# Tile 0's attention scores as plain float32 products over 64 rows, with a new table of priorities

## The chip, the cores and the metric

The kernel runs on one core of a Trainium2 chip. Five engines work side by side, each through its own instruction stream in order: TensorE (PE, with its weight loads PEld), VectorE (DVE), ScalarE (ACT), GpSimd (POOL) and SyncE (SP, which here only issues DMA transfers). The metric is the device time of one execution in microseconds (us).

## What is computed

Attention over 2 batches, 8 heads, 576 positions and 64 dimensions, in which every query keeps its 32 largest scores, and then two MLPs over the 1152 rows of 512 numbers. Everything is float32.

```python
scores = scale * np.matmul(q, k.transpose(0, 1, 3, 2))
kth = np.partition(scores, -32, axis=-1)[..., -32:-31]
scores = np.where(scores >= kth, scores, -1000000000.0)
attn = softmax(scores);  x = attn @ v          # per head, then (1152, 512)
h = x @ w_in;  g = h * tanh(softplus(h));  x = g @ w_out     # first MLP, d_ff 2048
x = (x @ w_a) * (x @ w_b) @ w_out                            # second MLP, d_ff 1536
```

## The kernel before

**Tiles.** The 1152 queries are nine tiles of 128; tile 4 holds the last 64 of each batch. A tile's attention is done for two heads at a time, a *pair* here: four pairs a tile, 36 in all, so pair 16 is the last of tile 3 and pair 26 the second of tile 6.

**Scores.** q and k come from memory transposed and twice over, in rows 0 to 63 and again in rows 64 to 127. A float32 product is made of two faster products in the format float32r: `prep_k` casts a head's k to float32r (line 347) and replaces rows 64 to 127 by what the cast lost (a subtraction, line 352), which gives the tile `kk`; `prep_q` makes `qh`, the cast of a pair's q, and `ql`, what it lost. `qh` times `kk` plus `ql` times `kk`, over 128 rows, is the score (line 468); each head is done in two halves of 288 columns, in a PSUM tile `psc`. ACT scales it into SBUF (line 473). Casts may go to ACT or DVE, subtractions to POOL or DVE.

**Search.** `largest` finds the 32 largest of 576 scores on DVE: for each of the two heads four times MAX8 (line 487) and between them three times MATCH_REPLACE8 (line 491), 8 and 6 instructions for a pair. Then ACT makes the masked exponentials (lines 530 and 533), PE transposes them (line 544, `pe`), ACT copies them, and PE multiplies them with v (lines 556 and 560, `px`).

**Weights.** They come as 64-bit numbers, 68 pieces (512 KB each). ACT takes one half of each word (line 624), ACT or POOL the other (lines 629, 631), POOL or DVE shift and add (lines 637 to 643), and the result is kept and also stored for a second use.

**MLPs.** Tiles 0, 1 and 2 go through the first MLP alone in plain float32 (`single`, products `ph` on line 784, then `acc` on line 714); tiles 3 to 5 and 6 to 8 in threes, with weights and activations split into two float32r parts (`gated`, lines 691, 712, 714); the second MLP (`bilinear`) goes in threes. Between the products of the first MLP stands `gate`: ACT, a minimum on POOL or DVE (line 745), three ACT steps and a DVE step (line 751).

**Order.** The program is a list of operations with priorities (`ATT`, `CONV`, `MLP`, `BIAS`). A planner (`Plan.run`) goes through a model of the engines, gives every free engine the ready operation with the smallest priority, chooses an engine where two are allowed (with the offsets `SHIFT` and `LOCKED`), and emits every engine's stream in that order. On the chip each stream is then followed to the letter: an instruction whose input is late holds up all behind it.

**What the change touches.** `RAW` names the tiles whose scores are done without `prep_q` and `prep_k`; the code for it is there, and the tuple is empty. `since` says at which tile a batch's k is prepared, the first that is not in `RAW`.

```python
since = [next(t for t in range(J + 1) if t not in RAW), J]
nc.tensor.matmul(psc()[:, :HS], QQ[t]()[:D, 2 * hp + s, :],
                 KR[b, hp]()[:D, s, a * HS:(a + 1) * HS], start=True, stop=True)
```

Of the kernel before, what the change touches and what calls it, by code (L numbers as in the profile page):

```python
# [26 lines left out]

SEQ = [(1, (0,), 0), (1, (1,), 0), (1, (2,), 0), (2, (0, 1, 2), 1), (1, (3, 4, 5), 1), (2, (3, 4, 5), 1),
       (1, (6, 7, 8), 1), (2, (6, 7, 8), 1)]
ATT = (-95.1, -36.4, 51.3, 93.5, 275.2, 298.4, 324.7, 574.5, 287.8, 2117.2)  # L30
CONV = (-156.2, -1.4, 50.6, 349.2, 528.4)
MLP = ((60.7, 126.0, -326.6, 1269.9), (97.8, 294.8, 551.3, -22.1), (-647.9, -146.1, -100.4, 111.3), (358.9, 501.8),
        (675.0, -3.6), (808.8, 2780.7), (965.3, 651.3), (-178.3, 7.5))
BIAS = {'scores': -43.1, 'search': 54.2, 'weigh': 49.7, 'gate': -708.6, 'conv': -16.9, 'load': 116.8, 'split':
        -23.9, 'x': -164.4, 'k': -304.6, 'prod': -25.3, 'acc': -7.7, 'out': -162.6, 'store': 620.6, 'v': 1161.1,
        'px': -671.5, 'mask': 337.5, 'turn': -20.1, 'tail': -26.6, 'last': 3.3, 'rest': 181.1}
FRESH = 200
RAW = ()
KEEP = (2, 2, 2, 2, 3, 3, 3, 3)
AHEAD = 1500.0  # L40
SLACK = 2500.0
# [25 lines left out]
class Plan:  # L67
# [11 lines left out]
    def add(self, engines, prio, fn, reads=(), writes=(), also=()):  # L79
        o = Op()  # L80
        o.engines, o.prio, o.fn, o.index = engines, round(prio, 3), fn, len(self.ops)
        o.need, o.bufs = set(), []
        touched = dict.fromkeys(also)
        for b, part in reads:
            for z in ([part] if part is not None else list(b.last)):
                if z in b.last:
                    o.need.add(b.last[z])
                elif None in b.last:
                    o.need.add(b.last[None])
                b.read.setdefault(z, []).append(o.index)  # L90
            if part is not None and None in b.last:
                o.need.add(b.last[None])
            touched[b] = None
        for b, part in writes:
            for z in ([part, None] if part is not None else list(b.last)):
                if z in b.last:
                    o.need.add(b.last[z])
            for z in ([part] if part is not None else list(b.read)):
                o.need.update(b.read.pop(z, []))
            if part is None:  # L100
                b.last.clear()
            b.last[part] = o.index
            touched[b] = None
        for b in touched:
            if not b.users:
                b.loaded = "SP" in engines
            b.users += 1
            o.bufs.append(b)
        o.need.discard(o.index)
        self.ops.append(o)  # L110
        return o
# [158 lines left out]

LAG = {"PE": 200.0, "DVE": 135.0, "ACT": 150.0, "POOL": 110.0, "SP": 2400.0}
START = {"PE": 900.0, "DVE": 900.0, "ACT": 2000.0, "POOL": 1700.0, "SP": 720.0}
SHIFT = {'DVE': -13.3, 'POOL': -36.4, 'ACT': 1362.4, 'PE': 0, 'SP': 0}
LOCKED = 720.9


def ramp(knots, z):
# [6 lines left out]
def topk_attention_mlps(ctx: ExitStack, tc: tile.TileContext, q, k, v, vr, w, out):  # L284
# [23 lines left out]
    add = plan.add  # L308
# [130 lines left out]
    def scores(t, hp, at):  # L439
        pr = at + BIAS["scores"]  # L440
        if hp == 0:
# [165 lines left out]
    for t, hp in steps:  # L607
        at = ATT[t] + (ATT[t + 1] - ATT[t]) * hp / NP
        s2 = scores(t, hp, at)
# [7 lines left out]
    for u, key in enumerate(order):  # L617
        pr = ramp(CONV, u / len(order)) + BIAS["conv"]
        w64 = buf("wp", [P, U], mybir.dt.int64, "w64", CAPS["w64"])
# [121 lines left out]
    def gate(pr, ph, full, N):  # L741
        e, g = buf("ep", [P, N], F32, f"e{N}", CAPS["ep"]), buf("ep", [P, N], F32, f"m{N}", CAPS["ep"])
        add(one("ACT", 75.0 + 0.83 * N), pr, lambda _: nc.scalar.activation(e(), ph()[:, :N], AF.Exp), full, [(e, 0)])
        add({"POOL": (95.0 + 1.22 * N, True), "DVE": (70.0 + 0.52 * N, True)}, pr,
            lambda z: ENG[z].tensor_scalar(e(), e(), TOP, None, op0=ALU.min), [(e, 0)], [(e, 0)])  # L745
        for cost, dst, fn, kw in ((110, e, AF.Square, {"bias": 1.0}), (200, e, AF.Ln, {"bias": half, "scale": 0.5}),
                                  (110, g, AF.Exp, {"scale": -1.0})):
            add(one("ACT", cost + 0.84 * N), pr,
                lambda _, dst=dst, fn=fn, kw=kw: nc.scalar.activation(dst(), e(), fn, **kw), [(e, 0)], [(dst, 0)])  # L749
        add(one("DVE", 65.0 + 1.04 * N), pr,  # L750
            lambda _: nc.vector.scalar_tensor_tensor(g(), g(), 1.0, ph()[:, :N], op0=ALU.subtract, op1=ALU.mult),
            full + [(g, 0)], [(g, 0)])
        return g
# [15 lines left out]
    def single(z, t, y):  # L769
        base = lambda f: MLP[z][0] + (MLP[z][1] - MLP[z][0]) * f / F1  # L770
        pre = lambda i: MLP[z][2] + (MLP[z][3] - MLP[z][2]) * i / (NC * FB)
        after = lambda c: ready(t, c - 1) if c else ready(t - 1) if t else []
# [24 lines left out]
    def gated(z, tiles, ys, direct):  # L797
        n = len(tiles)
        T = n * P
        base = lambda f: MLP[z][0] + (MLP[z][1] - MLP[z][0]) * f / F1  # L800
        xt = [buf("xp", [P, NC, T], F32R, f"x{y}{T}") for y in "hl"]
# [142 lines left out]
```

## Time and profile before

| | |
|---|---|
| median of 3 runs | 655.56 us (655.47 to 656.84) |
| the profiled execution | 654.66 us, its span 652.9 us |
| PE, PEld busy | 605.6, 532.8 us |
| DVE, ACT, POOL busy | 562.2, 470.5, 446.6 us |
| search on DVE, lines 487 and 491 | 205.0 and 159.1 us |
| `ph`, `po` and `acc` of the threes on PE, lines 691 and 714 | 231.8, 80.9, 85.5 us |

The span runs from the first to the last instruction of the profiled execution; 1.8 us of its own time lie around it. A busy PE is not a PE at its peak, since matmuls overlap and their ends are modelled; how close two starts stand tells its pace. A MAX8 and the next instruction overlap a little too, so that sums are made from durations only where the same kinds are compared.

### The profile page before, as it was taken

The numbers are of one execution on the slowest core, as the hardware profiler recorded it, in microseconds if no ns is written. First come the engines' busy times: TensorE is split into PE (matmuls) and PEld (weight loads), VectorE is DVE, ScalarE is ACT, GpSimd is POOL, SyncE is SP. The second block draws the span as 40 slices with busy tenths as digits, with TensorE's granted clock in tenths as the row PEclk, the third lists the DMA queues.
The fourth block names the chain that finished last, engine by engine and source line by source line (L and its number), as shares of the span: only waits on it lengthen the run. The fifth ranks groups of instructions, "written<-read, shape, count | busy, mean of one in ns | idle before, by whom it ended". The sixth has DMA issues, their size and how long they took to land.

```text
span 652.9 us, 12119 instructions
## 1 busy us (share of the span) xinstructions
PE 605.6 (93%) x4000; PEld 532.8 (82%) x4000; DVE 562.2 (86%) x1104; ACT 470.5 (72%) x1045; POOL 446.6 (68%) x485
## 2 busy tenths in 40 slices
PE   1488779999899999999999999999999999999997
PEld 1377646966757999898998997889999999999996
DVE  6999989989999999999999999997865788755552
ACT  4687899898999989998899789866542666432221
POOL 6999999988789999999887886453422566521110
PEclk9999899999999999999999999999999999999999
DMA  8887868978998755565753343133324444434401
GB/s 330 309 272 230 289 188 288 327 257 265 335 316 272 259 166 169 184 210 163 227 157 118 100 126 106 42 98 98 113 73 145 154 130 130 130 113 122 125 30 48
DMA packets 64719, 117.71 MB, mean 180 GB/s; under 512 B 6800, under 2 KB 23312, under 8 KB 64656
## 3 DMA queue, kind: packets, MB, share of 16 engines
q1 hardware_dynamic: 64512, 116.81, 55.4%
q8 instruction: 31, 0.51, 0.3%
q14 instruction: 32, 0.26, 0.1%
q10 hardware_dynamic: 144, 0.13, 0.1%
HBM read 96.73 MB, written 20.19 MB: 179 GB/s over the span
## 4 chain that ended last, share of the span: by engine, by line
PE 63%; DVE 15%; POOL 9%; ACT 6%; issue 3%; DMA 3%; SPq 0%; POOLq 0%; DVEq 0%; ACTq 0%
PE ph L691 30%; PE po L714 11%; DVE arena L487 6%; DVE arena L491 5%; PE acc L714 5%; PE acc L712 4%; PE psc L468 3%; PE pe L544 3%; PE px L556 3%; POOL arena L643 3%; PE ph L784 2%; ACT arena L347 2%; POOL arena L639 2%; DMA arena<-in_k_dram 1%; POOL arena L631 1%
## 5 line engine op out<-in xcount | busy, mean ns | idle before, releaser
L352 POOL TENSOR_TENSOR arena<-arena,arena 128x512 fp32r<-128x512 f32 (+3 forms) x192 | 221.3, 1164 | 151.4 <-ACT arena L347 97.2
L691 PE MATMUL ph<-arena 128*128 128x384 f32 x1248 | 231.8, 337 | 1.4 <-DVE arena L833 0.8
L691 PEld LDWEIGHTS ph<-arena 128*128 128x128 f32 x1248 | 216.9, 188 | 5.0 <-DVE arena L833 1.1
L487 DVE MAX8 arena<-arena 128x8 f32<-128x576 f32 x288 | 205.0, 745 | 2.4 <-ACT arena L473 1.8
L491 DVE MATCH_REPLACE8 arena<-arena 128x576 f32<-128x576 f32 x216 | 159.1, 740 | 0.1
L347 ACT CAST arena<-arena 128x512 fp32r<-128x512 f32 (+4 forms) x204 | 109.5, 558 | 51.0 <-PE ph L691 19.6
L352 DVE TENSOR_TENSOR arena<-arena,arena 128x512 fp32r<-128x512 f32 (+4 forms) x110 | 88.2, 802 | 11.8 <-ACT arena L347 8.1
L468 PE MATMUL psc<-arena 128*128 128x288 f32 x320 | 71.3, 343 | 22.3 <-POOL arena L352 14.9
L714 PE MATMUL acc<-arena 128*128 128x512 f32 x240 | 85.5, 478 | 4.5 <-issue 3.0
L643 POOL TENSOR_TENSOR arena<-arena 128x512 int32<-128x512 int32 x63 | 82.8, 1317 | 2.5 <-DVE arena L637 0.5
L714 PE MATMUL po<-arena 128*128 128x512 f32 x324 | 80.9, 394 | 0.0
L468 PEld LDWEIGHTS psc<-arena 128*128 128x128 f32 x320 | 51.0, 200 | 36.0 <-POOL arena L352 17.3
L347 DVE CAST arena<-arena 128x512 fp32r<-128x512 f32 (+2 forms) x98 | 52.2, 535 | 29.9 <-PE po L714 11.4
L714 PEld LDWEIGHTS po<-arena 128*128 128x128 f32 x324 | 59.5, 188 | 11.4 <-issue 0.3
L639 POOL TENSOR_TENSOR arena<-arena,eight 128x512 uint32<-128x512 uint32 x61 | 63.7, 1050 | 5.0 <-ACT arena L624 4.1
L749 ACT ACTIVATE arena<-arena 128x384 f32<-128x384 f32 (+1 forms) x88 | 48.2, 553 | 25.8 <-POOL arena L745 18.6
L530 ACT ACTIVATE arena<-arena 128x576 f32<-128x576 f32 x72 | 55.2, 783 | 9.8 <-DVE arena L487 8.8
L473 ACT ACTIVATE arena<-psc 128x288 f32<-128x288 f32 x144 | 54.4, 420 | 6.1 <-PE psc L468 5.4
L533 ACT ACTIVATE arena<-arena 128x576 f32<-128x576 f32 x72 | 56.0, 782 | 3.2 <-POOL arena L526 3.2
L784 PEld LDWEIGHTS ph<-arena 128*128 128x128 f32 x384 | 47.9, 200 | 8.9 <-DVE arena L581 5.7
L784 PE MATMUL ph<-arena 128*128 128x128 f32 x384 | 50.2, 286 | 3.9 <-DVE arena L581 3.4
L544 PEld LDWEIGHTS pe<-ident,arena 128*128 128x128 f32 x324 | 39.7, 145 | 16.3 <-ACT arena L533 6.5
(57 smaller groups left out, 698.6 us busy)
## 6 DMA issues: line engine op xcount, KB each, us to landing
arena<-ws SPq DMA_DIRECT2D x140, 256.0 KB, 2.7
arena<-in_w_dram SPq DMA_DIRECT2D x68, 512.0 KB, 5.1
ws<-arena SPq DMA_DIRECT2D x52, 256.0 KB, 5.2
arena<-wsa SPq DMA_DIRECT2D x48, 256.0 KB, 3.3
wsa<-arena SPq DMA_DIRECT2D x16, 256.0 KB, 5.2
arena<-in_q_dram SPq DMA_DIRECT2D x8, 512.0 KB, 5.4
arena<-in_k_dram SPq DMA_DIRECT2D x7, 576.0 KB, 4.4
arena<-in_v_dram SPq DMA_DIRECT2D x4, 512.0 KB, 6.8
```

The costliest lines, as they stand in the source:

```text
L347: add(eng, prio, lambda e: nc.scalar.copy(dst(), src()) if e == "ACT" else nc.vector.tensor_copy(dst(), src()), reads, writes)
L352: lambda e: ENG[e].tensor_sub(dst(), a(), b()), reads, writes)
L468: nc.tensor.matmul(psc()[:, :HS], z()[:, s, :], kk()[:, a * HS:(a + 1) * HS], start=(i == 0), stop=(i == len(heads) - 1))
L487: lambda e, s=s, src=src, got=got: nc.vector.max(m8()[:, s, got], src()[:, s, :]),
L491: lambda e, s=s, src=src, got=got: nc.vector.match_replace(wk()[:, s, :], m8()[:, s, got], src()[:, s, :], NEG),
L533: lambda e, s=s: nc.scalar.activation(e2()[:, s, :], e2()[:, s, :], AF.Exp, scale=-STEEP, bias=dm()[:, s - 2 + n:s - 1 + n], accum_out=at_ ...
L544: nc.tensor.transpose(pe()[:, i * P:(i + 1) * P], ef[:, n * P:(n + 1) * P], ident)
L639: nc.gpsimd.tensor_tensor(wi().bitcast(U32), wi().bitcast(U32), eight.to_broadcast([P, U]), op=ALU.mult)
L643: lambda e, word=word, wi=wi: ENG[e].tensor_tensor(wi(), wi(), word(I32, 0), op=ALU.add),
L691: nc.tensor.matmul(ph()[:, o:o + T], a, x, start=(i == 0), stop=(i == len(mm) - 1))
L714: nc.tensor.matmul(acc[i](), z[:, i * P:(i + 1) * P], a, start=begin, stop=end)
L784: nc.tensor.matmul(ph()[:, j * P:(j + 1) * P], wa()[:, j * P:(j + 1) * P], x()[:, c, :], start=(c == 0 and j == 0), stop=(c == NC - 1 and ...
```

## The change

Tile 0's scores are made as one plain float32 product over rows 0 to 63 of q and k as they lie (line 458), instead of two float32r products over 128 rows. So tile 0 needs no `qh`, `ql` and `kk`. The k of batch 0 is loaded in two halves, rows 0 to 63 for tile 0 and rows 64 to 127 for `prep_k`, which now belongs to tile 1; the raw k of batch 0 stays in four tiles of their own. Of tile 0's q only rows 0 to 63 are loaded. The planner's price of the minimum on POOL (line 745) rises from 95 + 1.22 to 100 + 2.27 ns a column, and all priorities are new.

```diff
-ATT = (-95.1, -36.4, 51.3, 93.5, 275.2, 298.4, 324.7, 574.5, 287.8, 2117.2)
+ATT = (-57.5, -46.3, 47.6, 83.9, 224.8, 264.3, 487.1, 592.9, 528.3, 2195.4)
...
-RAW = ()
+RAW = (0,)
...
-SHIFT = {'DVE': -13.3, 'POOL': -36.4, 'ACT': 1362.4, 'PE': 0, 'SP': 0}
-LOCKED = 720.9
+SHIFT = {'DVE': 30.3, 'POOL': -17.2, 'ACT': 2219.2, 'PE': 0, 'SP': 0}
+LOCKED = 972.4
...
-        add({"POOL": (95.0 + 1.22 * N, True), "DVE": (70.0 + 0.52 * N, True)}, pr,
+        add({"POOL": (100.0 + 2.27 * N, True), "DVE": (70.0 + 0.52 * N, True)}, pr,
             lambda z: ENG[z].tensor_scalar(e(), e(), TOP, None, op0=ALU.min), [(e, 0)], [(e, 0)])
```

`CONV`, `MLP` and `BIAS` change in the same way as `ATT`.

In the rows that follow, `arena_81` is SBUF in float32 and `arena_82` SBUF in float32r; the line number tells the step. DVE at the start of the program, before:

```order
L347 CAST arena_82<-arena_81 128x576
L352 TENSOR_TENSOR arena_82<-arena_81,arena_82 64x576
L347 CAST arena_82<-arena_81 128x256
L352 TENSOR_TENSOR arena_82<-arena_81,arena_82 128x256
L637 TENSOR_SCALAR arena_81<-arena_81 128x512
L487 MAX arena_81<-arena_81 128x8
L347 CAST arena_82<-arena_81 128x256
L491 MATCH_REPLACE arena_81<-arena_81 128x576
L487 MAX arena_81<-arena_81 128x8 x2
```

and now:

```order
L487 MAX arena_81<-arena_81 128x8
L491 MATCH_REPLACE arena_81<-arena_81 128x576
L487 MAX arena_81<-arena_81 128x8 x2
L491 MATCH_REPLACE arena_81<-arena_81 128x576
L352 TENSOR_TENSOR arena_82<-arena_81,arena_82 64x576
L491 MATCH_REPLACE arena_81<-arena_81 128x576
L487 MAX arena_81<-arena_81 128x8
L352 TENSOR_TENSOR arena_82<-arena_81,arena_82 64x576
L347 CAST arena_82<-arena_81 128x576
L487 MAX arena_81<-arena_81 128x8
L491 MATCH_REPLACE arena_81<-arena_81 128x576
L352 TENSOR_TENSOR arena_82<-arena_81,arena_82 64x576
```

The search comes first; five of the eight subtractions of k (64x576), of which three are shown, and one of its casts now stand inside the first pair's search; the fourth stands ahead of its sixth MAX8, the fifth ahead of its seventh. ACT at the start of the program, before; the copies from `psc` are the scaled scores, the casts of 128x576 are k:

```order
L347 CAST arena_82<-arena_81 128x576
L347 CAST arena_82<-arena_81 128x256
L624 ACTIVATE arena_81<-arena_81 128x512
L473 ACTIVATE arena_81<-psc 128x288 x3
L624 ACTIVATE arena_81<-arena_81 128x512
L473 ACTIVATE arena_81<-psc 128x288
L629 ACTIVATE arena_81<-arena_81 128x512
```

and now:

```order
L473 ACTIVATE arena_81<-psc 128x288 x4
L347 CAST arena_82<-arena_81 128x576
L473 ACTIVATE arena_81<-psc 128x288
L347 CAST arena_82<-arena_81 128x576
L473 ACTIVATE arena_81<-psc 128x288
L347 CAST arena_82<-arena_81 128x576
L473 ACTIVATE arena_81<-psc 128x288 x3
L347 CAST arena_82<-arena_81 128x576
L473 ACTIVATE arena_81<-psc 128x288 x2
L347 CAST arena_82<-arena_81 128x576
L473 ACTIVATE arena_81<-psc 128x288 x2
L624 ACTIVATE arena_81<-arena_81 128x512
```

Behind these rows come three more copies, a sixth cast of k, a piece of weights (line 624) and a seventh cast of k. So all four pairs' scores of tile 0 and seven of the eight casts of k stand in a row, where before the first pair's four copies were followed by weights. SP's transfers at the start of the program, the difference:

```order
-L341 DMA arena_81<-in_k_dram 128x576 x2
-L341 DMA arena_81<-in_q_dram 128x768
+L341 DMA arena_81<-in_k_dram 64x576 x2
+L341 DMA arena_81<-in_q_dram 64x768
+L341 DMA arena_81<-in_k_dram 64x1152 x3
+L341 DMA arena_81<-in_k_dram 64x576 x2
+L341 DMA arena_81<-in_k_dram 64x1152 x3
 L341 DMA arena_81<-in_w_dram 128x512 x4
```

The whole k of batch 0, in ten loads of 64 rows, now stands ahead of the first four pieces of weights; before, three quarters of it came behind them.

## Rows read from the trace of the kernel before

**Rows 1.** Windows: stretch, length, busy PE, PEld, DVE, ACT, POOL (instructions), clock, DMA, GB/s.

```profile
0.00:100.00 100.00, 64.47 (x431) 51.14 (x432) 90.54 (x188) 75.99 (x164) 89.06 (x106) 0.98 0.81 271
...
225.00:653.00 428.00, 421.20 (x2730) 389.73 (x2728) 349.88 (x666) 281.23 (x630) 246.97 (x240) 1.00 0.41 127
```

**Rows 2.** Timeline: start, duration, engine, line; ends of pairs 16 and 26, their transposes.

```profile
205.35 0.75 DVE L487 MAX8 arena<-arena 128x8 f32<-128x576 f32 x1
...
204.76 4.26 PE L691 MATMUL ph<-arena 128*128 128x384 f32 x23 [0.19 <-DVE arena L738]
208.94 0.55 PE L544 MATMUL pe<-ident,arena 128*128 128x128 f32 x3
...
318.31 0.76 DVE L487 MAX8 arena<-arena 128x8 f32<-128x576 f32 x1
...
324.17 1.14 PE L544 MATMUL pe<-ident,arena 128*128 128x128 f32 x9
```

**Rows 3.** Timeline of the first 45 us, DVE, POOL and PE.

```profile
4.35 0.46 DVE L347 CAST arena<-arena 128x576 fp32r<-128x576 f32 x1 [3.44 <-DMA arena<-in_k_dram]
...
8.95 0.76 DVE L487 MAX8 arena<-arena 128x8 f32<-128x576 f32 x1 [0.17 <-ACT arena L473]
...
21.03 0.75 DVE L487 MAX8 arena<-arena 128x8 f32<-128x576 f32 x1
...
8.55 0.75 POOL L631 TENSOR_SCALAR arena<-arena 128x512 int32<-128x512 uint32 x1
...
37.35 5.49 PE L784 MATMUL ph<-arena 128*128 128x128 f32 x24 [2.09 <-DVE arena L581]
...
43.81 1.05 PE L784 MATMUL ph<-arena 128*128 128x128 f32 x8
```

**Rows 4.** DMA issues: transfer, queue, count, size, median us from issue to landing.

```profile
arena<-in_q_dram ACTq DMA_DIRECT2D x1, 128.0 KB, 3.8
```

**Rows 5.** The chain that ended last, in time: start, us, group.

```profile
122.25 3.57 PE ph L784 x32
...
144.06 1.72 PE acc L714 x4
...
235.56 2.10 PE ph L691 x12
```

**Rows 6.** Groups by line and shape: count, busy us, mean ns, idle before.

```profile
L473 ACT ACTIVATE arena<-psc 128x288 f32<-128x288 f32 x144 | 54.4, 420 | 6.1 <-PE psc L468 5.4
...
L352 DVE TENSOR_TENSOR arena<-arena,arena 128x512 fp32r<-128x512 f32 x66 | 46.6, 706 | 5.2 <-ACT arena L347 2.0
...
L352 DVE TENSOR_TENSOR arena<-arena,arena 128x384 fp32r<-128x384 f32 x29 | 29.2, 1008 | 6.2 <-ACT arena L347 6.1
...
L855 DVE TENSOR_TENSOR arena<-ph,arena 128x384 f32<-128x384 f32 x36 | 19.8, 551 | 22.1 <-PE ph L691 20.8 <-ACT arena L533 0.9
...
L352 POOL TENSOR_TENSOR arena<-arena,arena 64x576 fp32r<-64x576 f32 x9 | 12.9, 1433 | 5.8 <-ACT arena L347 4.5 <-POOL arena L745 0.5 <-POOL arena L352 0.4
...
L352 DVE TENSOR_TENSOR arena<-arena,arena 64x576 fp32r<-64x576 f32 x7 | 6.5, 922 | 0.2
...
L347 DVE CAST arena<-arena 128x576 fp32r<-128x576 f32 x9 | 5.2, 589 | 3.5 <-DMA arena<-in_k_dram 3.4
L347 ACT CAST arena<-arena 128x576 fp32r<-128x576 f32 x7 | 4.6, 676 | 5.8 <-DMA arena<-in_k_dram 5.8
L745 DVE TENSOR_SCALAR arena<-arena 128x512 f32<-128x512 f32 x7 | 4.6, 665 | 1.0 <-ACT arena L743 1.0
L352 DVE TENSOR_TENSOR arena<-arena,arena 128x256 fp32r<-128x256 f32 x6 | 4.2, 707 | 0.0
```

**Rows 7.** DVE's waits from 20 to 330 us: us in total, times, longest.

```profile
DVE arena L571 <- POOL arena L569: 1.7, 1, 1.7
DVE arena L751 <- ACT arena L749: 1.6, 2, 1.2
```

**Rows 8.** DMA from 511 to 520 us: GB/s in 40 slices.

```profile
GB/s 0 0 0 0 0 0 328 364 391 82 0 0 0 25 200 237 287 371 408 276 273 200 264 328 373 200 36 18 0 0 0 0 0 0 0 0 173 155 264 391
```

More of the change, by code (lines that the diff above doesn't have):

```diff
@@ L29 @@
        (1, (6, 7, 8), 1), (2, (6, 7, 8), 1)]
-ATT = (-95.1, -36.4, 51.3, 93.5, 275.2, 298.4, 324.7, 574.5, 287.8, 2117.2)
[L31 to L36, printed above, removed]
+ATT = (-57.5, -46.3, 47.6, 83.9, 224.8, 264.3, 487.1, 592.9, 528.3, 2195.4)
+CONV = (-140.8, -86.9, 24.7, 360.8, 543.5)
+MLP = ((-40.1, 108.8, -575.7, 1231.5), (242.2, 338.3, 237.0, -38.4), (-815.0, -200.1, -416.0, 215.1), (330.5,
+        577.2), (822.0, -59.3), (853.8, 2338.1), (555.5, 390.4), (-120.5, -19.1))
+BIAS = {'scores': -62.1, 'search': 66.5, 'weigh': 33.0, 'gate': -840.9, 'conv': -48.4, 'load': -341.5, 'split':
+        -64.5, 'x': -151.1, 'k': -594.8, 'prod': 27.2, 'acc': 36.1, 'out': -108.6, 'store': 555.4, 'v': 1257.1,
+        'px': -641.9, 'mask': 1083.0, 'turn': -16.7, 'tail': -0.1, 'last': -0.2, 'rest': 556.3}
 FRESH = 200
-RAW = ()
+RAW = (0,)
 KEEP = (2, 2, 2, 2, 3, 3, 3, 3)
```

## The prediction

> **What bounds the kernel now.** I read the windows first, then the timeline at the ends of searches, then the start.
>
> The windows show where time is lost [rows 1]. In the first 100 us PE is busy for 64.5, from 225 us on for 421.2 of 428. DVE is busy for 90.5 of the first 100. So PE is the bound of the later two thirds, and what it did not get to do in the front is missing at the end.
>
> The timeline shows where DVE sets PE's pace [rows 2]. The search of pair 16 ends at 205.35 + 0.75 = 206.1; PE works on `ph` right up to 208.94 and then starts the transposes of that pair, 2.8 us after the search. Between them lie two ACT passes over each head, so I take 2.8 as about the least there can be: here DVE and PE meet. At pair 26 the search ends at 319.1 and the transposes start at 324.17, 5.1 later: 2.3 us of slack. From the start of pair 16's transposes to the end it is 652.9 - 208.9 = 444.0 us. In the orders of both kernels PE's instructions from that point to the end are the same in number, kind for kind (1224 `ph` of 384 columns, 324 `po`, 192 and 144 `acc`, 160 `psc`, 189 transposes and the small ones). From pair 26 on the new order has six `psc` products fewer. So the change in time is the change in when DVE ends these searches, less slack, as long as PE is not later for reasons of its own.
>
> **The change part by part.** I call X the change of the end of the first pair's search, now at 21.03 + 0.75 = 21.8 [rows 3].
>
> *The products of tile 0.* Sixteen float32 products of 288 columns come, 32 float32r ones go. A float32 product is two records in the trace: 32 records of 128 columns take 3.57 us, 111 ns each, and 4 of 512 take 1.72, 430 each [rows 5]; 288 columns lie at about 244, so 0.49 us a product. The float32r products are bounded from above by those of 384 columns, 2.10/12 = 0.175 [rows 5], and 288/384 of that is 0.13. PE's work grows by 16 x 0.49 - 32 x 0.13 = 3.6 us. It all lies in the first 20 us, where PE waits for most of the time [rows 1], and costs nothing; without that cover it costs 3.6. [...]
>
> *The start of the search.* Before, k lands, DVE casts it at 4.35, and after cast, subtraction, product and copy MAX8 starts at 8.95 [rows 3]. Now the first product waits for half of k's first head and a load of q, issued at 0.8 and about 3.8 us under way [rows 4]: 4.6. Two products at 0.98, 0.2 for the end of the second (an estimate) and one copy of 0.42 [rows 6]: MAX8 starts at 7.2. The pair's own search is (205.0 + 159.1)/36 = 10.1 by the profile table. Into it the new order puts five subtractions of k at 0.92 and one cast at 0.59 [rows 6], 5.2 us. Without a wait it ends at 22.5: X = +0.7.
>
> *Waits in it.* The fourth subtraction in DVE's stream needs a cast that stands on ACT behind all 16 copies, five other casts and one piece of weights. DVE gets to it after 10 of 14 search steps, three subtractions and a cast, 7.2 + 7.2 + 3.4 = 17.8. ACT, never held up, has done it at 5.8 + 16 x 0.42 + 7 x 0.68 = 17.3 [rows 6]: no wait. [...] X lies between +0.7 and +4.3. ACT's first cast, after the fourth copy at 9.1, needs rows 64 to 127 of k, behind 1.4 MB of 64-row loads. The trace has two 64-row stores at about 515.3 to 516.2 us; in these slices 276, 273, 200 and 264 GB/s move, 371 and 408 ahead of them [rows 8], about 0.6. At 245 GB/s the rows land at 10.2 and hold ACT for 1.1, and DVE for 0.6. I take 0.7 for all waits, so **X = +1.4**.
>
> [...]
>
> *The rest of DVE's work.* Counted in the two orders, between the first pair and pair 16 two casts of k (0.59), one subtraction of q (0.71) and one of k (0.92) go, a minimum (0.67) and a short cast (0.3, an estimate) come [rows 6]: -1.9 us. Between the first pair and pair 26 three such casts and the two subtractions go (-3.4), two subtractions of 128x384 (1.01) and two of 128x512 (0.71), a minimum and a gate product (0.55) come (+4.7), and short casts and differences add 0.3: +1.5.
>
> *The other queues.* SP issues eleven loads ahead of the weights instead of three. POOL's first weight step, at 8.55 [rows 3], moves behind three subtractions of k (1.43 each) and, by the loads, to about 16. The first `ph` products ran at 37.35 [rows 3]; a delay of 7.5 us is covered if POOL converts four pieces in the 21 us that are left. Were it not, PE would start later by what is missing; it has 35 us of idle time in the front to absorb it. POOL later has two subtractions of k and three minima less, so it catches up. v lands at about 22 and is wanted behind the first transposes, at 26. The dearer minimum moves three of 44 from POOL to DVE; those that matter are counted above. Four output copies move from DVE to ACT, where neither is the bound: nothing.
>
> *The sum.* At pair 16: X - 1.9 = -0.5. At pair 26: X + 1.5, less 0.8 for six `psc` products that PE no longer has behind it, less the slack of 2.3: X - 1.6 = -0.2. The larger decides: -0.2. The profiled execution took 654.66, its span 652.9, and the median is 0.9 above it; I take the change from the median: **655.4**. With X at its ends it is 654.7 to 658.3, waits elsewhere aside.
>
> **The rivals.**
>
> *Faster: DVE's waits go too.* Up to pair 26 DVE waits for a reciprocal behind POOL (1.7) and twice for ACT's gate (1.6) [rows 7]. POOL has less to do and the gate's minimum moves to DVE, which speaks for it; that the streams are all new, and may bring waits like these elsewhere, against it. With X = +0.7 and one or both waits gone it is -0.9 - 1.6 to -0.9 - 3.3, so 651.4 to 653.1, at the middle 652.2. It decides if pair 16's transposes start before 207.6.
>
> [...]
>
> *Slower: the new work shows.* If PE does not fill the front better than before, because weights come late or scores wait for casts, it is not DVE that sets the pace, and the 3.6 us come on top: 659.2. Against it speaks that all of batch 0's k is prepared early now.
>
> **How the numbers follow.** A measurement of this kernel can tell about 0.2%, 1.3 us, from no change. Forecast, from 654.3 to 656.8: 0.35. Faster through fewer waits: 0.34. Slower through the front: 0.23. Slower through PE's own work: 0.08. So faster 0.34, same 0.35, slower 0.31. All streams are reordered, and a wait of 2 or 3 us on DVE before pair 26 shows in full, so the rivals are wide: the range takes in the middle of the fast rival with both waits gone, 651.4, and the slowest case, 659.4.
>
> **What would show it.** The first MAX8 at 7.2; the end of the first pair's search at 23.2; its fourth subtraction of k waiting for ACT by less than 1 us; pair 16's transposes at about 208.4 and pair 26's at about 323.5; PE's gaps after 225 us as small as before. I am wrong on the front if the first pair ends after 24.7 or before 22; wrong on the method if PE starts pair 16's transposes more than 5 us after that search, which means that PE is late on its own, or if the stretch behind it is not within 1.5 us of 444.

## The result, and the profile after

The changed kernel takes 659.61 us in the median of 19 executions, the kernel before, run beside it, 655.37: a ratio of 1.0051, with a 95% interval from 1.0036 to 1.0067. Slower by 0.5%, and just outside the range (651.4 to 659.4). The median alone hides something: the 19 executions stand in two groups, 14 from 658.5 to 660.6 and five from 654.6 to 656.1, with nothing between, while 18 of the 19 before lie within 2.5 us and the last at 657.4. The forecast, 655.4, is where the small group is. The profiled execution is of the large one (659.63, span 657.8).

The windows of after, in the stretches of [rows 1] (stretch, length, busy PE, PEld, DVE, ACT, POOL with their instructions, clock, DMA share, GB/s):

```profile
0.00:100.00 100.00, 76.46 (x465) 60.60 (x466) 89.26 (x182) 78.84 (x173) 80.38 (x101) 0.93 0.81 250
...
225.00:658.00 433.00, 422.51 (x2733) 389.92 (x2731) 350.70 (x660) 286.41 (x641) 247.93 (x240) 1.00 0.41 130
```

PE fills the front better than before (34 more instructions by 100 us), but from 225 us on it is idle for 10.5 us where it was idle for 6.8. The timeline of after where [rows 2] stood, the ends of the searches of pairs 16 and 26 and their transposes:

```profile
205.82 1.41 DVE L487 MAX8 arena<-arena 128x8 f32<-128x576 f32 x2
...
205.95 4.26 PE L691 MATMUL ph<-arena 128*128 128x384 f32 x23 [1.49 <-DVE arena L738]
210.05 0.49 PE L544 MATMUL pe<-ident,arena 128*128 128x128 f32 x3
...
324.57 2.73 DVE L487 MAX8 arena<-arena 128x8 f32<-128x576 f32 x4
...
329.77 1.41 PE L544 MATMUL pe<-ident,arena 128*128 128x128 f32 x9
```

The first of the two MAX8 ends pair 16, at 206.6 (before 206.1); the second of the four ends pair 26, at 326.0 (before 319.1). The transposes are 1.1 and 5.6 later than in [rows 2], and the span is 4.9 longer. So nearly all of it is lost between these two places. Pair by pair the searches run level with before up to pair 23 (286.5 against 286.8), and pair 24's ends at 302.9 against 298.0. The timeline between them, DVE, then POOL, PE and ACT:

```profile
295.06 0.75 DVE L487 MAX8 arena<-arena 128x8 f32<-128x576 f32 x1
295.74 5.15 DVE L352 TENSOR_TENSOR arena<-arena,arena 128x384 fp32r<-128x384 f32 x1
...
294.93 2.60 POOL L643 TENSOR_TENSOR arena<-arena 128x512 int32<-128x512 int32 x2
297.48 1.06 POOL L639 TENSOR_TENSOR arena<-arena,eight 128x512 uint32<-128x512 uint32 x1
298.48 0.76 POOL L352 TENSOR_TENSOR arena<-arena,arena 128x256 fp32r<-128x256 f32 x1
299.18 1.30 POOL L643 TENSOR_TENSOR arena<-arena 128x512 int32<-128x512 int32 x1
...
300.94 0.98 PE L714 MATMUL po<-arena 128*128 128x512 f32 x3 [1.56 <-DVE arena L352]
...
302.38 1.44 ACT L530 ACTIVATE arena<-arena 128x576 f32<-128x576 f32 x2 [3.60 <-DVE arena L487]
```

One subtraction takes 5.15 us, where the other 27 of its shape take 0.54 to 1.45. It counts as busy, so that no list of waits shows it. The group's mean (count, busy us, mean ns, idle before) hides it too: it is about that of [rows 6], since the others are shorter, 0.88 in the mean:

```profile
L352 DVE TENSOR_TENSOR arena<-arena,arena 128x384 fp32r<-128x384 f32 x28 | 29.0, 1035 | 8.1 <-ACT arena L347 8.0
```
 
The subtraction ends at 300.89, 0.41 behind the last of five GpSimd instructions (2, 1, 1 and 1 in the rows) that follow each other without a gap and have two inputs each. PE (1.56) and ACT (3.60) wait for what stands behind it.

The front, where the prediction had put its risk, in the timeline of after (PE, ACT, DVE):

```profile
4.04 15.70 PE L458 MATMUL psc<-arena 64*128 64x288 f32 x32 [4.04 <-DMA arena<-in_k_dram]
...
7.29 0.41 ACT L473 ACTIVATE arena<-psc 128x288 f32<-128x288 f32 x1 [0.55 <-PE psc L458]
...
10.56 0.67 ACT L347 CAST arena<-arena 128x576 fp32r<-128x576 f32 x1 [1.90 <-DMA arena<-in_k_dram]
...
6.77 0.76 DVE L487 MAX8 arena<-arena 128x8 f32<-128x576 f32 x1 [5.86 <-ACT arena L473]
...
12.13 1.25 DVE L352 TENSOR_TENSOR arena<-arena,arena 64x576 fp32r<-64x576 f32 x1 [1.57 <-ACT arena L347]
...
20.77 0.76 DVE L352 TENSOR_TENSOR arena<-arena,arena 64x576 fp32r<-64x576 f32 x1 [1.05 <-ACT arena L347]
...
23.91 1.41 DVE L487 MAX8 arena<-arena 128x8 f32<-128x576 f32 x2
```

The two MAX8 at 23.91 end the first pair's search, at 25.3: X = +3.5, not +1.4.

### The profile page after: what moved, and what is told of

It is laid out like the page before. It is cut to its first block, busy times and chain, and to the rows that moved or that the text cites. A ratio compares the mean times of both kernels' runs of the same rounds, so it can differ in the third digit from the quotient of the medians.

```text
span 657.8 us, 12073 instructions
## 1 busy us (share of the span) xinstructions
PE 616.3 (94%) x4000; PEld 538.3 (82%) x4000; DVE 562.4 (85%) x1095; ACT 473.2 (72%) x1048; POOL 442.1 (67%) x483
## 4 chain that ended last, share of the span: by engine, by line
PE 70%; DVE 13%; POOL 5%; ACT 4%; issue 2%; DMA 1%; SPq 0%; POOLq 0%; ACTq 0%
PE ph L691 30%; PE po L714 10%; PE acc L714 7%; DVE arena L491 5%; PE acc L712 5%; DVE arena L487 5%; PE ph L784 4%; PE psc L468 4%; PE px L556 4%; PE pe L544 4%; POOL arena L643 2%; POOL arena L639 1%; DVE arena L352 1%; ACT arena L347 1%; PE prs L597 1%
## 5 line engine op out<-in xcount | busy, mean ns | idle before, releaser
L352 POOL TENSOR_TENSOR arena<-arena,arena 128x512 fp32r<-128x512 f32 (+4 forms) x188 | 217.5, 1170 | 162.3 <-ACT arena L347 101.8
L691 PEld LDWEIGHTS ph<-arena 128*128 128x128 f32 x1248 | 216.8, 188 | 6.2 <-DVE arena L738 1.8
L347 ACT CAST arena<-arena 128x512 fp32r<-128x512 f32 (+4 forms) x207 | 111.8, 557 | 48.0 <-PE ph L691 19.7
L352 DVE TENSOR_TENSOR arena<-arena,arena 128x512 fp32r<-128x512 f32 (+4 forms) x110 | 92.0, 838 | 16.9 <-ACT arena L347 13.4
L639 POOL TENSOR_TENSOR arena<-arena,eight 128x512 uint32<-128x512 uint32 x62 | 65.6, 1064 | 7.7 <-ACT arena L624 6.7
L468 PE MATMUL psc<-arena 128*128 128x288 f32 x288 | 60.3, 335 | 9.2 <-POOL arena L352 7.5
L347 DVE CAST arena<-arena 128x512 fp32r<-128x512 f32 (+3 forms) x91 | 43.1, 479 | 28.9 <-PE po L714 12.8
L468 PEld LDWEIGHTS psc<-arena 128*128 128x128 f32 x288 | 45.2, 200 | 18.6 <-POOL arena L352 8.6
L714 PEld LDWEIGHTS acc<-arena 128*128 128x128 f32 x240 | 42.2, 190 | 21.8 <-issue 7.3
L544 PE MATMUL pe<-ident,arena 128*128 128x128 f32 x324 | 48.1, 283 | 8.7 <-ACT arena L533 8.7
```

The costliest lines, as they stand in the source:

```text
L347: add(eng, prio, lambda e: nc.scalar.copy(dst(), src()) if e == "ACT" else nc.vector.tensor_copy(dst(), src()), reads, writes)
L352: lambda e: ENG[e].tensor_sub(dst(), a(), b()), reads, writes)
L468: nc.tensor.matmul(psc()[:, :HS], z()[:, s, :], kk()[:, a * HS:(a + 1) * HS], start=(i == 0), stop=(i == len(heads) - 1))
L544: nc.tensor.transpose(pe()[:, i * P:(i + 1) * P], ef[:, n * P:(n + 1) * P], ident)
L639: nc.gpsimd.tensor_tensor(wi().bitcast(U32), wi().bitcast(U32), eight.to_broadcast([P, U]), op=ALU.mult)
L691: nc.tensor.matmul(ph()[:, o:o + T], a, x, start=(i == 0), stop=(i == len(mm) - 1))
```

## The experiments

Theory: the front costs what DVE's first search is late, DVE's other waits give most of it back, and the 4 us that separate the two groups of executions are the one subtraction at 295.7. Rivals: PE's own 3.6 us of new products show at the end; or the front alone is the loss. Each kernel is the changed one with the edit that is shown, and each was timed against the kernel before, which took 655.1 to 655.6 in the median beside them. Additions shift line numbers by a few. Of the 35 executions of the kernel before beside the first four runs, one took 660.63, as long as the upper group; it was not profiled, so whether the kernel before can lose time at a place of this kind is not shown.

| kernel | median us | ratio to before, 95% interval |
|---|---|---|
| hold: GpSimd held for the subtraction | 655.57 | 0.9985 to 1.0017 |
| copy: its control | 655.94 | 1.0005 to 1.0022 |
| whole: k in 128-row loads | 657.16 | 1.0014 to 1.0056 |
| quick: products in one pass | 656.30 | 1.0010 to 1.0049 |
| clear: hold, whole and quick | 651.86 | 0.9934 to 0.9961 |
| early: hold, 2.8 us more DVE work up to pair 14 | 655.93 | 1.0000 to 1.0019 |
| later: hold, the same in pairs 29 to 32 | 655.45 | 0.9988 to 1.0012 |
| moved2, moved4: hold and whole, subtractions to GpSimd | 656.25, 655.94 | 0.9999 to 1.0021, 1.0003 to 1.0025 |
| shift16: hold, subtractions later | 656.95 | 1.0007 to 1.0027 |
| pull: hold, search earlier | 654.57 | 0.9981 to 1.0001 |

**GpSimd held for the subtraction, and the control.**

```diff
+    late = [o for o in started if "DVE" in o.engines][432]
+    held_up = [o for o in started if "POOL" in o.engines][308]
...
+    def behind(e):
+        nc.gpsimd.tensor_copy(spot, late.bufs[-1]()[:, :1].bitcast(F32))
+        fn(e)
+
+    held_up.fn = behind
```

> The changed kernel, with one thing added: at 296 us GpSimd, before its second weight addition (line 643), copies one column of what DVE's subtraction of 128x384 (line 352, 5.15 us at 295.74) writes, so that GpSimd has to wait for that subtraction. Theory: the subtraction is kept out of SBUF by four GpSimd instructions in a row, and the 4 us that most executions lose are this one wait. Then the subtraction takes under 1.2 us, pair 24's search ends at about 298.7 rather than 302.9, and the time is 655.6, with no execution near 659.6. Rival (the loss is the front, or PE's own 3.6 us of products): the time stays at 659.6 in most executions.

The control reads the constant `half` instead.

> The control to the run before: the same GpSimd copy at the same place, but of a constant, so that GpSimd waits for nothing. Theory that the wait for GpSimd is the loss: most executions stay at about 659.7, the subtraction at 295.7 takes 4 to 5.5 us in them. Rival (one instruction more is enough to let DVE in, or the loss has nothing to do with this place): 655.6 in the first case, and the same as the run before in the second.

With GpSimd held, the 12 executions lie from 654.7 to 657.0: the upper group is gone. DVE and POOL in it, and under them the same two of the control:

```profile
295.22 0.94 DVE L352 TENSOR_TENSOR arena<-arena,arena 128x384 fp32r<-128x384 f32 x1
...
296.22 0.19 POOL L903 COPY spot<-arena 128x1 f32<-128x1 f32 x1 [0.48 <-DVE arena L352]
```

```profile
296.79 0.95 DVE L352 TENSOR_TENSOR arena<-arena,arena 128x384 fp32r<-128x384 f32 x1
...
297.24 0.54 POOL L903 COPY spot<-half 128x1 f32<-128x1 f32 x1
```

The subtraction takes 0.94, pair 24 ends at 298.2, and the time is that of the small group. So the 4 us are this wait, and PE's 3.6 us of new products, which are still in this kernel, are not the loss. The control went against what I expected and as its rival said: all its 12 executions are from 655.6 to 656.9, the subtraction takes 0.95, and it is the one-column copy that waits (0.54 rather than 0.19). Holding GpSimd is not needed; in this place a short copy between the two additions was enough to let DVE in. In both kernels the long wait is gone together with the upper group.

**The loads and the products of the front.**

```diff
-            dma(pr, lambda h=h, n=n: kr()[part(z), h:h + n], lambda h=h, n=n: k[b, part(z), 2 * hp + h:2 * hp + h + n, :],
+            if b == 0 and RAW and z == 1:
+                add(one("SP", size), pr, lambda e: None, done, [(kr, (z, h))])
+                continue
+            rows = slice(0, P) if b == 0 and RAW else part(z)
+            dma(pr, lambda h=h, n=n: kr()[rows, h:h + n], lambda h=h, n=n: k[b, rows, 2 * hp + h:2 * hp + h + n, :],
```

> The changed kernel with batch 0's k loaded in 128 rows at the places of the 64-row loads for tile 0; the loads of rows 64 to 127 are left out, as they are in. Theory that 64-row loads run at half the rate (205 to 235 GB/s against 394 to 430 in the kernel before): the DMAs move about 400 GB/s from 4 to 11 us, the first cast of k on ACT at 9.0 instead of 10.56, weights 3.5 us earlier, the first pair's search ends 1 to 2 us earlier (23.3 to 24.3 instead of 25.3); the time falls by 0.5 to 1.5 against executions of the changed kernel with the same wait at 296. Rival (PE's slow products set the front, not the loads): the first pair ends within 0.5 of 25.3, the time stays.

```diff
-                        nc.tensor.matmul(psc()[:, :HS], QQ[t]()[:D, 2 * hp + s, :],
-                                         KR[b, hp]()[:D, s, a * HS:(a + 1) * HS], start=True, stop=True)
+                        top = lambda x: x.bitcast(mybir.dt.bfloat16).rearrange("p (n t) -> p n t", t=2)[:, :, 1]
+                        nc.tensor.matmul(psc()[:, :HS], top(QQ[t]()[:D, 2 * hp + s, :]),
+                                         top(KR[b, hp]()[:D, s, a * HS:(a + 1) * HS]), start=True, stop=True)
```

> The changed kernel with the 16 products of tile 0 made from the upper 16 bits of q and k only, in one pass instead of two, which leaves out the lower bits; everything else stands in the same order. Theory (the front counts through DVE alone): the products end by about 13 instead of 19.7, the first pair's search at 22.5 to 23.5 instead of 25.3, pair 16's transposes 1 to 2.5 earlier, the time 1 to 2.5 lower against executions with the same wait at 296. Rival (PE's own work shows): the time falls by the whole 3.6 us or more. Second rival (all of the front is absorbed): no change.

Neither moved the front: the first pair's search ends at 25.8 with whole loads and at 25.3 with quick products. What ACT waits for in each tells why, first with whole loads, then with quick products:

```profile
7.64 0.41 ACT L478 ACTIVATE arena<-psc 128x288 f32<-128x288 f32 x1 [0.55 <-PE psc L463]
...
8.91 0.66 ACT L347 CAST arena<-arena 128x576 fp32r<-128x576 f32 x1
```

```profile
10.57 0.67 ACT L347 CAST arena<-arena 128x576 fp32r<-128x576 f32 x1 [4.55 <-DMA arena<-in_k_dram]
```

With whole loads the first cast no longer waits for k, but the later casts still stand behind copies that come 0.96 apart, at PE's pace; with quick products the copies are done and the cast waits 4.55 for rows 64 to 127. Their medians say little, since both keep the place at 296 us as it was: whole has six executions of 12 from 658.3 up and six from 654.5 to 656.0, quick four from 660.0 up and eight from 654.9 to 657.3. Their profiles tie the lower group to a short subtraction: it takes 2.19 in the profiled execution with quick products (656.27) and 0.92 in that with whole loads (656.00), while the changed kernel's profiled execution, with 5.15, is of the upper group. With whole loads:

```profile
296.48 0.92 DVE L352 TENSOR_TENSOR arena<-arena,arena 128x384 fp32r<-128x384 f32 x1
```

The products' own work made no difference: the quick ones leave the lower group of executions where it was. That speaks against the rival of PE's 3.6 us once more.

The kernel with GpSimd held, with both of these edits added:

> The run in which GpSimd is held at 296 us, with both of the others in it: k in 128-row loads, and tile 0's products from the upper 16 bits in one pass (the lower bits are left out). Alone neither moved the first pair's search from 25.3 to 25.8. Theory: each hides the other (with whole loads ACT waits for products 0.96 apart, with quick products it waits 4.55 for rows 64 to 127), so with both gone the first pair's search ends at 21 to 22.5, pair 16's transposes at 206 to 208 instead of 209.6, and the time is 652.5 to 654.5 against 655.57. Rival (what the front loses is made good by fewer waits up to pair 16 anyway): the first pair ends early but pair 16 stays within 0.7 of 209.6, the time within 0.5 of 655.57.

```profile
21.11 2.07 DVE L494 MAX8 arena<-arena 128x8 f32<-128x576 f32 x3
...
207.25 0.49 PE L551 MATMUL pe<-ident,arena 128*128 128x128 f32 x3
```

The second of the three MAX8 ends the first search, at 22.5. Pair 16's transposes start at 207.25 against 209.61 with GpSimd held alone, which is 3.5 behind the search in both, so it is the search that moved them. PE's last product comes 2.2 earlier, and the time is 3.7 lower (six executions, 650.5 to 652.3; interval 2.6 to 4.3 below before). So loads and products cover for each other, and what the front loses does come through. This kernel leaves out the lower bits of tile 0's scores and is no answer for use.

**DVE work added before and behind the places where it should count.** Both have GpSimd held; the first has `range(10, 14)`, the second `range(28, 32)`.

```diff
+    for p in range(10, 14):
+        o = searches[8 * p + 4]
...
+            fn(e)
+            fn(e)
```

> The run in which GpSimd is held at 296 us, with one MAX8 done twice in each of pairs 11 to 14: 2.8 us more work for DVE before pair 16, nothing else. Theory (DVE's search sets PE's pace at pairs 16 and 26): pair 16's search and transposes 2.5 to 2.8 later than 206.1 and 209.6, the time 1.5 to 2.8 above 655.57, so 657.1 to 658.4. Rival (PE is late on its own): under 0.7 more.

> The same 2.8 us of DVE work, but in pairs 29 to 32, from 353 to 416 us, where PE starts a pair's transposes 15 to 30 us behind its search. Theory: it is hidden, the time within 0.5 of 655.57. Rival (DVE bounds up to pair 36): up to 2.8 more, 658.4.

Of 2.8 us of early work, 1.0 came through: pair 16's search ends at 207.1 and its transposes start at 210.61 against 209.61 with GpSimd held alone, PE's last product comes 1.1 later, and the median is 0.36 higher, with intervals that overlap. DVE's waits between 125 and 206 us, 1.7 without the extra work, are 0.5 with it. So my expectation of 1.5 to 2.8 was too high: pair 16's transposes move with DVE's search, but waits in its stream swallow 1.2 of what is added, and the rest of the difference is not accounted for. The late work moved the median by -0.12, as expected; but in its profile PE's last product is 1.1 later too, behind pairs 31 and 32. From the start of that product to the end it is 4.3 to 5.6 us in different executions, so that single profiles do not separate about 1 us. By the time alone, then, these two runs do not show that early work counts more than late work; what shows it is where the transposes moved.

**What lets GpSimd go ahead.** Three kernels add trials behind the end of the program: a row of five GpSimd instructions, and one subtraction on DVE that begins in another phase of the first of them each time. The first had 28 trials, the second 64, the third 80.

```diff
+            row()
+            nc.vector.max(ff(11, 8), f[:, 512 * 8:512 * 8 + 876 + 4 * k])
+            nc.vector.tensor_sub(gl, ff(9, 384), ff(10, 384))
```

> The changed kernel with 28 trials behind its end, so its time is longer by what they take: five GpSimd instructions in a row with two inputs in SBUF (14 times the five kinds that stood in a row at 296 us, 14 times five additions on one tile), and beside them on DVE a MAX8 of growing length and then a subtraction of 128x384, so that it begins in another phase of the GpSimd instruction each time. Theory A: the subtraction always waits for the instruction that runs, and goes next: 0.4 to 1.7 us. Theory B (the next GpSimd instruction can go ahead of it again and again, as at 296 us): in some phases it takes 2 to 5 us, ending with the row.

> The changed kernel with 64 trials behind its end; its time is longer by them. Each has the row of five GpSimd instructions that stood at 296 us, and one subtraction of 128x384 on DVE that begins between 0.6 and 0.35 us before the end of the first of them, in steps of 5 ns: 40 times released by a copy on ACT, as at 296 us, 24 times behind a MAX8 on DVE. In the profiles so far the subtraction at 296 us waited past the next addition when it began 0.505 to 0.523 before the end (three profiles) and went in when it began 0.497 before (one). Theory A (a narrow window of the phase): a few trials near 0.51 take 2.2 to 5.2 us, the rest end 0.41 behind the first instruction. Theory B (it needs something else of that place): all trials end 0.41 behind the first instruction.

> The same trials as in the run before, with the phases that it left out: the subtraction begins between 0.57 and 0.43 us before the end of the first GpSimd instruction, 46 times released by ACT in steps of 2 to 3 ns, 34 times behind a MAX8 in steps of 4 ns. So far 92 trials outside that stretch all ended 0.41 to 0.43 behind the first instruction. Theory A (a narrow window of the phase, near 0.505 to 0.523, as in the three profiles in which the subtraction at 296 us waited on): several of these take 2.2 to 5.2 us. Theory B (it needs something else of that place): all end 0.41 behind.

Two trials of the first (DVE, then POOL), and the subtraction at 296 us in the same profile:

```profile
675.69 1.58 DVE L913 TENSOR_TENSOR arena<-arena 128x384 fp32r<-128x384 f32 x1
...
675.60 2.79 POOL L903 TENSOR_TENSOR arena<-arena 128x512 int32<-128x512 int32 x2
...
719.00 0.85 DVE L913 TENSOR_TENSOR arena<-arena 128x384 fp32r<-128x384 f32 x1
...
718.17 2.80 POOL L903 TENSOR_TENSOR arena<-arena 128x512 int32<-128x512 int32 x2
```

```profile
295.44 5.13 DVE L352 TENSOR_TENSOR arena<-arena,arena 128x384 fp32r<-128x384 f32 x1
```

In 167 of the 172 trials the subtraction began 0.13 to 1.20 before the end of a running GpSimd instruction. In all of these it ended 0.41 to 0.43 behind that one, and it was the next GpSimd instruction that grew (the two additions together take 2.79 rather than 2.5). In none did it wait past a second. In the other five it met no GpSimd instruction, or only the last 0.06 of one, and took 0.54. At 296 us, in the six profiles in which the place is as in the changed kernel, it waited past four more (5.15, 5.13, 4.96 and 5.13 us), past one more (2.19, with quick products) and past none (0.92, with whole loads). It began 0.50 to 0.52 before the end of the instruction that ran in five of them, and 0.34 before it in the one with 4.96. The second and third sets of trials went through these phases, and none waited on. So it is not the phase alone. One difference was not tried: at 296 us two multiplications run on GpSimd right ahead of the addition that the subtraction meets, in the trials the row begins with that addition. What lets GpSimd go ahead was not found and stays open.

**Versions meant to be faster.** All have GpSimd held. Two of the first search's subtractions given to GpSimd, and four (`(1, 2, 3, 4)` in place of `(3, 4)`), with whole loads:

```diff
+    kept = [o for o in started if o.engines.get("DVE", (0,))[0] == 70.0 + 1.04 * S and o.bufs[-1].name == "kk"]
+    for i in (3, 4):
+        kept[i].engines = {"POOL": (100.0 + 2.27 * S, True)}
```

> A version meant to beat both: GpSimd held at 296 us, k of batch 0 in 128-row loads, and two of the five subtractions of k that stand inside the first pair's search (the fourth and fifth) done by GpSimd instead of DVE, at the same place of the program. Theory (what the front delays the search comes through one for one): DVE loses 2 x 0.92 of work and a wait of 1 to 1.85 there, the first pair's search ends at 22 to 23.2 instead of 25.8, the time 652.5 to 654 against 655.5. Rival (GpSimd, 2.8 us later with its weights, holds the first products instead): 655 to 657.

> The same with four of the five subtractions (second to fifth) on GpSimd. Theory: the first pair's search ends at 20 to 21.5, the time 651 to 653. Rival (GpSimd's weights come 5.6 us later and the scores of tile 1 wait for its subtractions): PE's first product of the MLP later than 40 us, no gain over the run with two moved, or slower than 655.5.

The first search did end earlier, at 23.4 and 19.2, but the rival won: GpSimd's small steps stood behind the subtractions, and DVE waited for one of them inside the second pair's search (in the profile with two moved):

```profile
35.41 0.17 DVE L577 RECIPROCAL arena<-arena 128x2 f32<-128x2 f32 x1 [3.99 <-POOL arena L575]
```

The second pair's search ended 2.1 and 1.7 later than with GpSimd held alone; no run has whole loads and GpSimd held without the moves, so the part of the loads in this is not shown. Then the order of DVE's stream alone, first with the subtractions moved back:

```diff
+    todo = [(o, search[max(16 - 1, done - 1) if 16 > 0 else done - 1 - 16]) for o, (_, done) in zip(kept, seen)]
+    for o, z in reversed(todo):
+        old = started.index(o)
+        started.pop(old)
+        new = started.index(z) + 1
+        started.insert(new, o)
```

> GpSimd held at 296 us, k in halves and products as in the changed kernel, but DVE's five subtractions and one cast of k moved out of the first pair's search, behind its end and two MAX8 of the second pair. Their inputs are there by then (the last cast on ACT ends at 20.7). Theory (what the front costs is DVE's waits in that search, 2.6 us, and each us comes through): the first pair's search ends at 16.8 to 17.5, the second pair's at 33.5 to 34.5 instead of 36.2, pair 16's at 204 to 205 instead of 206.1, the time 653 to 654.5 against 655.57. Rival (fewer waits there are made good by more elsewhere): pair 16 within 0.5 of 206.1 and the time within 0.5 of 655.57.

In this kernel one head's cast of k comes behind the GpSimd subtraction that belongs to it, so that head's scores are made from other numbers; the work is the same. A subtraction that stands behind later loads in the program now waits, by the profile, for one of them, of v, which it does not read:

```profile
23.01 1.40 DVE L352 TENSOR_TENSOR arena<-arena,arena 64x576 fp32r<-64x576 f32 x1 [4.52 <-DMA arena<-in_v_dram]
```

The second pair ended 2.2 later, pair 16 3.0 later, and the median was 1.4 higher, with intervals that overlap. It did not answer the question, but in its profile a late second pair is not made good by pair 16. The next one pulls the search ahead instead, and leaves subtractions and loads in their places:

```diff
+    ahead(search[:12], kept[0])
+    ahead(kept[2:3], kept[0])
+    ahead(search[12:14], kept[0])
+    ahead(search[14:16], kept[4])
```

> GpSimd held at 296 us, loads and products as in the changed kernel; in DVE's stream the rest of the first pair's search, and two MAX8 of the second pair, stand ahead of the subtractions of k instead of behind them (the run before moved the subtractions back behind later loads and so made them wait 4.5 us for one; here their loads stay as they are). Theory: DVE no longer waits 2.6 us for casts, the first pair's search ends at 17 to 18, the second pair's at 33.5 to 34.5 instead of 36.2, pair 16's at 203.5 to 205 instead of 206.1, the time 652.5 to 654 against 655.57, below both kernels. Rival (the third subtraction, the cast and what hangs on them come later, and GpSimd's weights with them): the second pair ends at 36 or later and the time is 655.5 or more.

```profile
17.45 3.39 DVE L352 TENSOR_TENSOR arena<-arena,arena 64x576 fp32r<-64x576 f32 x3
...
22.32 2.52 DVE L352 TENSOR_TENSOR arena<-arena,arena 64x576 fp32r<-64x576 f32 x2
```

The waits of 2.6 are gone. Half of it is paid back, since five subtractions that follow each other beside a busy GpSimd take 5.9 instead of 4.7; the second pair ends 1.5 earlier (34.7), pair 16 1.2 earlier, and the time is 654.57, 5.0 below the changed kernel. It is 1.0 below that with GpSimd held, but the intervals overlap, and against the kernel before, 0.9981 to 1.0001, it is not told apart.

## Why the prediction was wrong

**The step that failed** is in the rest of DVE's work: every subtraction was taken at the mean of its row, 1.01 for 128x384 [rows 6], and one took 5.15 in most executions. I had written that a wait of 2 or 3 us on DVE before pair 26 shows in full; I had no mechanism for it on the slow side: the slowest case worked out was 659.2, and the range ended at 659.4. The signs named for being wrong were there: the stretch behind pair 16's transposes is 657.8 - 210.05 = 447.8, not within 1.5 of 444, and the first pair ends at 25.3, after 24.7. With that wait gone the kernel takes 655.57, for a forecast of 655.4: from hold to the changed kernel's profile, pair 24's search moves by 4.7, pair 26's transposes by 4.5 and the span by 4.7.

**That the kernel without this wait comes so close to 655.4 is partly luck**, and the profile with GpSimd held shows what cancelled.

*The end of the first search.* X was to be +1.4 and is +3.5. MAX8 starts at 6.77, 0.4 earlier than forecast. The five subtractions and the cast take 1.25 + 0.76 + 1.19 + 0.76 + 0.76 + 0.46 = 5.2, as forecast. The waits are 1.57 + 1.05 = 2.6 and not 0.7, and what is left for the 14 steps of the search is 25.3 - 6.77 - 5.2 - 2.6 = 10.7 and not 10.1. So the mis-sized term was the waits, taken at 0.7 together: the first subtraction waited 1.57, where the working gave 0.6, and the fourth 1.05, where it gave none, or 3.6 at the upper end of X. PE did all 32 records of its products in 15.70 us, 0.49 each, at a granted clock of 1.00. The 0.98 us a product in the working for MAX8's start, and the +4.3 at the upper end of X, were my estimates for a PE that is slow throughout: no run shows what would make it slow, and the profile shows the pace alone, two records of 0.49 a product. And the half loads were slower than the 0.6 that I took. The DMA rows of one window (stretch, length, clock, DMA share, GB/s), after and before:

```profile
6.00:7.00 1.00, 1.00 1.02 212
```

```profile
6.00:7.00 1.00, 1.00 1.05 430
```

From 3 to 15 us it is 205 to 235 where it was up to 430, about a half, and ACT's first cast waited 1.90, not 1.1. My rows [rows 8], two stores among other transfers, did not show it in full. But the run with whole loads shows that this was not what the front hung on alone.

*DVE's waits behind it.* Windows of 25 to 206 us, busy DVE, before and with GpSimd held:

```profile
25.00:206.00 181.00, 174.98 (x363) 0.99 0.85 282
```

```profile
25.00:206.00 181.00, 177.62 (x369) 0.94 0.86 284
```

In that stretch the list of waits has 5.0 us before ([rows 7] has the largest) and 2.7 with GpSimd held: the reciprocal's wait fell from 1.7 to 0.8, the gate's from 1.6 to 0.7. That is what my faster rival had described. By the windows DVE's idle time fell from 6.0 to 3.4, which takes in waits too short for the list. So at pair 16 the slow front (+3.6), less idle time (-2.6) and less work (-1.0 as the remainder; forecast -1.9, though the terms given for it add up to -1.8) add up to 0.0, forecast -0.5. A slower front and fewer waits came true at once, with opposite signs.

*From pair 16 on.* The transposes of pairs 16 and 26 with GpSimd held:

```profile
209.61 0.49 PE L545 MATMUL pe<-ident,arena 128*128 128x128 f32 x3
...
325.28 1.14 PE L545 MATMUL pe<-ident,arena 128*128 128x128 f32 x9
```

Pair 16's start 3.5 behind the search, where I took 2.8 for the least. Pair 26's start 1.1 later than before, where the working gave +0.6: of the 2.3 us of slack only 1.1 was to be had. Less 0.8 for the six products, it is +0.3; the spans differ by 0.2. The stretch behind pair 16's transposes is 653.1 - 209.6 = 443.5, within the 1.5 of 444 that I had named as the test. So without the long wait the way of the sum holds. That it meets the span to 0.1 is luck too: PE's last product starts 1.0 earlier than before, so PE gained 2.1 behind pair 26 and not 0.8, and the stretch from that product to the end is 1.2 longer, which is within what executions differ by there.

*PE's new work.* Taken as free, and free: the rival that put it on top gave 659.2, close to the measured median, but with the products still in and the one subtraction mended the time is 655.57. A right number from a wrong reason.

*The rest of the front* went as written or did not matter: PE's first `ph` products began no later than before, and the new order keeps PE fuller up to 100 us, a gain that is given back by pair 16, where DVE decides: by 200 us PE has done 1107 instructions, before 1111. No run separates the new priorities, the new way of scoring and the dearer GpSimd minimum from each other, so the share of each is not shown.

## What to carry to other kernels

When a DVE subtraction with two inputs in SBUF can meet a row of back-to-back GpSimd instructions, as at 296 us here, let the range take in a wait for the whole row (5.15 us for a step of 1.01), even if the forecast uses the mean; and look in a trace for single instructions far longer than their kind: such a wait counts as busy and stands in no list of waits. When executions of one kernel fall into two groups, ask what differs in one of them before explaining the median. When two causes hold the same step, taking away either one shows nothing, so try both together. When single profiles are compared, look first at how much a stretch differs between executions by itself (4.3 to 5.6 us behind the last product here).

## What the runs showed of the hardware

- In 167 trials a subtraction of 128x384 on DVE with both inputs in SBUF ended 0.41 to 0.43 us behind the GpSimd instruction that it met, and went ahead of the next. At 296 us it was otherwise: there the same subtraction was passed over by up to four GpSimd instructions that began after it and took 4.96 to 5.15 us in four of six profiles. No trial could bring that about.
- 64-row loads moved 205 to 235 GB/s at a DMA share of 0.91 to 1.10 (3 to 15 us of after); 128-row loads moved up to 430 (before).
- PE worked for 15.70 us without a pause on float32 products over 64 rows, and the records took 0.49 us each, twice the 0.24 worked out from records of 128 and 512 columns [rows 5], though the granted clock reads 1.00 (4 to 20 us of after). The 64 rows need not be the reason: nine transposes over 128 rows took 2.18 us at 27.42 and 1.20 at 42.76, at a granted clock of 1.00 both times. What sets the slower pace is not shown. Later the granted clock itself fell, after a stretch in which PE was busy for 3.14 of 7 us (windows of after, busy PE, clock):

```profile
43.00:50.00 7.00, 3.14 (x30) 0.96 0.71 215
...
54.00:58.00 4.00, 2.74 (x11) 0.50 0.86 253
```

It stood at 0.50 up to 63 us and again for 3.4 us near 131, where before it fell for 3.4 us only, near 70. What that cost was not tried by itself; the transposes of pairs 4 and 5, behind it, started 2.2 and 1.7 earlier than before.
